# Spreading the steps of a Sinkhorn iteration among matrix products of a fused attention, MLP and expert kernel

## The chip, the cores and the metric

The kernel runs on one core of a Trainium2 chip. The metric is the device time of one execution in microseconds (us); the kernel before was run three times for it. A profiled execution of the same program gives the trace that is read below. The engines are TensorE (PE for its matmuls, PEld for its weight loads), VectorE (DVE), ScalarE (ACT), GpSimd (POOL) and SyncE (SP), which issues the DMA transfers of this kernel.

## The reference

Three stages follow each other: attention with pooled keys and values, an MLP with ELU, and a mixture of eight experts whose gates are balanced by eight rounds of a Sinkhorn iteration.

```python
def _moe2_ref(x, w_gate, w1, w2):          # x: 2304 x 512, w1: 8 x 512 x 1024
    logits = x @ w_gate
    logits = logits - logits.max()
    P = np.exp(logits)
    for _ in range(8):
        P /= P.sum(1, keepdims=True) + 1e-09
        P /= P.sum(0, keepdims=True) + 1e-09
        P *= N / E
    out = np.zeros((N, D), dtype=np.float32)
    for e in range(E):
        h = np.maximum(x @ w1[e], 0.0)
        ye = h @ w2[e]
        out += P[:, e:e + 1] * ye
    return out
```

The gates `P` are used only in the last line, when an expert's output is added up. The product `x @ w1[e]` does not need them.

## The kernel before

The attention and the MLP run in one loop over `items`, 80 of them: five groups `g` of hidden chunks, five token tiles `t` (four of 512 tokens, one of 256), and the chunks of a group. Each item has the first MLP product (`layer1`, L527, tile `p_<item>`), its ELU (L539, L540 on ACT, L547 on DVE), a split into a high and a low part `h` (L548 on ACT, L549 on DVE), and, two items later, the second product (`layer2`, L560, tiles `p_<item>_<j>`). In the last group (g is 4, items 60 to 79) the outputs of a token tile are complete after its four items; `finish2` adds them into `x2a[t]` (L582 on DVE).

From there on work of a second kind exists, kept as a queue of Python generators named `side`. Each `yield` is a place where the queue can be left and entered again. `advance(n)` takes n steps from the front of the queue. For every token tile the queue gets `gate_tile(t)`, which computes the gate logits by matmuls of 8 columns (L442, tile `pg`), and some `halve(t, u)`, which split the tile into the high and low operands `xs` of the next stage (L628 on ACT, L629 on DVE, with differences at L639 to L648). After the last tile it gets `sinkhorn()`.

`sinkhorn()` takes the maximum of all logits (L459 on DVE, a transpose `pmx` at L462, `pmb` at L468 on PE), then the exponential (L471 on ACT), and then eight rounds. A round is a chain on DVE that normalises the rows (L476 to L479), one matmul with a matrix of ones that forms the column sums and gives them to all partitions (`pcs`, L483 on PE), and a chain on DVE that normalises the columns (L486 to L493). Each part needs the one before it.

The next stage, the first pass over the experts, forms `x @ w1[e]` by a scheme of seven products for four blocks. Its unit of work is a `Unit(i, u)`: weight pair i of 32 and token block u of 3. The products run in the order 1, 6, 3 of the unit before, 2, 7, 5, 4, six matmuls each (L713; banks `pa`, `pb`, `pc`, `pd`); product 7 adds to the bank `pb` after product 6 has been read from it (`read`, L732 on DVE), product 2 to `pa` after ACT has read product 1 (L729). Four units of pairs 0 and 1 come first, on token blocks 0 and 1, then pairs 0 and 1 on block 2, then pair 2 on the blocks 0, 1, 2, and so on. After each product the loop calls `advance(2)`. `need(u)` takes steps until the operands of block u exist. After the fifth unit (n is 4) the loop empties the queue:

```python
        if n == 2 * NUNIT - 2:
            advance(10**6)
            load_pair(2)
            load_pair(3)
```

The weights of a pair are loaded by SP (tile `rw`), combined on POOL (L683 to L686), and split into `w` by ACT (L690) and POOL (L691). All large tiles share 24 slots, so a load waits until another tile is given up.

The second pass multiplies by `w2` (L794) and applies the gates; it starts late in the run, and first reads the gates at 1286.8 us of the trace.

The code is written down in the order of these calls; a scheduler then orders each engine's instructions by that order and by what it takes to be ready. Afterwards each engine works through its list in order.

Of the kernel before, what the change touches and what calls it, by code (L numbers as in the profile page):

```python
# [17 lines left out]
def tile_attention_mlp_moe(  # L18
# [34 lines left out]
    E, _, F = w1.shape  # L53
# [14 lines left out]
    G0 = len(SPLIT)  # L68
# [5 lines left out]
    NUNIT = NT // 2 // UW  # L74
# [25 lines left out]
    def bank(name):  # L100
        return psum.tile([P, 512], F32, tag="ps", name=name)
# [326 lines left out]
    def advance_attention(upto):  # L428
        while tick[0] <= min(upto, max(ticks)):
            for step, u in ticks.get(tick[0], []):  # L430
                step(u)
            tick[0] += 1


    def gate_tile(t):
# [17 lines left out]
        )  # L453
        yield

    def sinkhorn():
        NS = NT // P
        mx = cpool.tile([P, 1], F32, name="gmx")
        nc.vector.reduce_max(mx, logits, axis=AX.XY)  # L459
        yield  # L460
        ps = bank("pmx")
        nc.tensor.transpose(ps[0:1, 0:P], mx, ident)  # L462
        m1 = cpool.tile([1, 1], F32, name="gm1")
        nc.vector.tensor_reduce(m1, ps[0:1, 0:P], axis=AX.X, op=ALU.max, negate=True)
        yield
        yield
        ps = bank("pmb")
        nc.tensor.matmul(ps[:, 0:1], ones[0:1, :], m1, start=True, stop=True)  # L468
        nm = cpool.tile([P, 1], F32, name="gnm")
        nc.vector.tensor_copy(nm, ps[:, 0:1])  # L470
        nc.scalar.activation(gates, logits, AF.Exp, bias=nm)  # L471
        rs = cpool.tile([P, NS, 1], F32, name="grs")
        cs = cpool.tile([P, 1, E], F32, name="gcs")
        yield
        for it in range(8):
            nc.vector.reduce_sum(rs, gates, axis=AX.X)  # L476
            nc.vector.tensor_scalar_add(rs, rs, 1e-9)  # L477
            nc.vector.reciprocal(rs, rs)
            nc.vector.tensor_mul(gates, gates, rs.to_broadcast([P, NS, E]))  # L479
            yield  # L480
            yield
            ps = bank(f"pcs{it}")
            nc.tensor.matmul(  # L483
                ps[:, 0 : NS * E], ones, gates.rearrange("p s e -> p (s e)"), start=True, stop=True
            )
            nc.vector.reduce_sum(  # L486
                cs.rearrange("p o e -> p (o e)").unsqueeze(2),
                ps[:, 0 : NS * E].rearrange("p (s e) -> p e s", e=E),
                axis=AX.X,
            )  # L490
            nc.vector.tensor_scalar_add(cs, cs, 1e-9)
            nc.vector.reciprocal(cs, cs)
            nc.vector.scalar_tensor_tensor(  # L493
                gates,
                gates,
                float(NT) / E,
                cs.to_broadcast([P, NS, E]),
                op0=ALU.mult,
                op1=ALU.mult,
            )  # L500
            yield
# [4 lines left out]
    def advance(n=1):  # L506
        for _ in range(n):
            while side:
                try:
                    next(side[0])  # L510
                    break
                except StopIteration:
                    side.pop(0)
# [60 lines left out]
    def finish2(g, t, ps):  # L574
        n = WIDTH[t]
        if g == 0:
            x2a[t] = slot([P, NC, n], F32, f"x2a{t}")
            for j in range(NC):
                nc.scalar.copy(x2a[t][:, j, :], ps[j][:, 0:n])
        else:  # L580
            for j in range(NC):
                nc.vector.tensor_add(x2a[t][:, j, :], ps[j][:, 0:n], x2a[t][:, j, :])  # L582
        if g == G0 - 1:
            del xh[t], xl[t]
            side.append(gate_tile(t))
            side.extend(halve(t, u) for u in AFTER[t])
            if t == NTILE - 1:
                side.append(sinkhorn())
# [7 lines left out]
    CUTS = {}  # L596
# [8 lines left out]
    made = set()  # L605
# [64 lines left out]
    def load_pair(i):  # L670
        e, f = pairs[i]
        raw1[i] = slot([P, 8, 2, P], F32, f"rw{i}")
        for place, hh, kh in ((A11, 0, 0), (A12, 0, 1), (A21, 1, 0), (A22, 1, 1)):
            o = (hh * NPAIR + f) * P
            nc.sync.dma_start(
                raw1[i][:, place],
                w1[e][kh * 2 * P : (kh + 1) * 2 * P, o : o + P].rearrange("(c p) f -> p c f", p=P),
            )

    def split_pair(i):  # L680
        raw = raw1.pop(i)
        g = nc.gpsimd
        g.tensor_add(raw[:, S1], raw[:, A21], raw[:, A22])  # L683
        g.tensor_sub(raw[:, S2], raw[:, S1], raw[:, A11])
        g.tensor_sub(raw[:, S3], raw[:, A11], raw[:, A21])  # L685
        g.tensor_sub(raw[:, S4], raw[:, A12], raw[:, S2])  # L686
        w1s[i] = [slot([P, 7, 2, P], F32R, f"w1{l}_{i}") for l in range(2)]
        for js in (slice(0, 3), slice(3, 5), slice(5, 7)):
            rs = slice(js.start + 1, js.stop + 1)
            nc.scalar.copy(w1s[i][0][:, js], raw[:, rs])  # L690
            g.tensor_sub(w1s[i][1][:, js], raw[:, rs], f32(w1s[i][0][:, js]))  # L691
# [61 lines left out]
    def load_w2(e, q):  # L753

        raw2[e, q] = slot([P, 2, 2, DM], F32, f"rv{e}_{q}")
        rows = w2[e].rearrange("(h f p) d -> f p h d", h=2, p=P)
        for i in range(2):
            nc.sync.dma_start(raw2[e, q][:, i], rows[2 * q + i])
# [81 lines left out]
    def pause(i, left):  # L840


        g, t, f = items[min(i, len(items) - 1)]
        rate = 0.0
        if g == 0:
            for u in range(t + 1, NTILE):
                runs = ((u - t) * SIZE[0] - f - 1) * 4 + left
                rate = max(rate, (ready[u] - tick[0] + 1) / max(runs, 1))
        credit[0] += rate
        n = int(credit[0])  # L850
        credit[0] -= n
        if n:
            advance_attention(tick[0] + n - 1)
        else:
            advance()

    def drive(gen, i, left):
        while True:
            try:
                next(gen)  # L860
            except StopIteration:
                return
            pause(i, left)
# [38 lines left out]
    for i in range(len(items) + LAG):  # L902
        if i < len(items):
            g, t, f = items[i]
            if g == 0:
                advance_attention(ready[t])
            if t == 0:
                finish_chunks(FIRST[g] + f)
            if (g, t, f) == (G0 - 1, NTILE - 1, 0):
                load_pair(0)  # L910
            drive(layer1(i), i, 3)
            pause(i, 2)
        if i >= LAG:
            drive(layer2(i - LAG), i, 1)
            pause(i, 0)
            finish1(i)
            g, t, f = items[i - LAG]
            if t == NTILE - 1:
                done.add(FIRST[g] + f)
            if i > 3:  # L920
                step_chunks()
        else:
            finish1(i)
        if i == len(items) - 2:
            split_pair(0)
            load_pair(1)


    def need(u):
        while not all(k in made for k in CUTS if k[1] == u):  # L930
            advance()
# [5 lines left out]
    for n, (i, u) in enumerate(order1):  # L937
        need(u)
        unit = Unit(i, u)
        for m in (1, 6, None, 2, 7, 5, 4):  # L940
            if m is not None:
                unit.product(m)
                unit.read(m)
            elif last is not None:
                last.product(3)
                last.read(3)
                if last.u == NUNIT - 1:
                    del w1s[last.i]
            advance(2)
        last = unit  # L950
        if n == 2 * NUNIT - 2:
            advance(10**6)
            load_pair(2)
            load_pair(3)
        if n >= 2 * NUNIT - 1 and u == NUNIT - 1 and i + 1 < len(pairs):
            split_pair(i + 1)
            if i + 3 < len(pairs):
                load_pair(i + 3)
        if (i, u) == (len(pairs) - 1, 0):
            load_w2(0, 0)  # L960
# [73 lines left out]
```

## Time and profile before

| | |
|---|---|
| three runs | 2053.34, 2054.75, 2055.7 us; median 2054.75 us |
| profiled execution | 2061.65 us, of which the span from first to last instruction is 2059.9 us |
| PE busy | 1996.6 us, 97% of the span |
| DVE, ACT, POOL busy | 49%, 33%, 20% |
| mean granted TensorE clock | 0.984 of full speed |
| place of the gates' iteration | 555.6 us (maximum of the logits) to 607.1 us (last column step) |

The times of a stage are read from the start of the span. Busy shares are averages over stages with different limits, so a stage has to be looked at by itself.

### The profile page before, as it was taken

The numbers are of one execution on the slowest core, as the hardware profiler recorded it, in microseconds if no ns is written. First come the engines' busy times: TensorE is split into PE (matmuls) and PEld (weight loads), VectorE is DVE, ScalarE is ACT, GpSimd is POOL, SyncE is SP. The second block draws the span as 40 slices with busy tenths as digits, with TensorE's granted clock in tenths as the row PEclk, the third lists the DMA queues.
The fourth block names the chain that finished last, engine by engine and source line by source line (L and its number), as shares of the span: only waits on it lengthen the run. The fifth ranks groups of instructions, "written<-read, shape, count | busy, mean of one in ns | idle before, by whom it ended". The sixth has DMA issues, their size and how long they took to land.

```text
span 2059.9 us, 27328 instructions
## 1 busy us (share of the span) xinstructions
PE 1996.6 (97%) x10139; PEld 1769.9 (86%) x10139; DVE 1008.5 (49%) x1877; ACT 671.9 (33%) x1361; POOL 408.2 (20%) x443
## 2 busy tenths in 40 slices
PE   4899999999969999999999999999999999999999
PEld 3578888888959999999999999888888888888887
DVE  7978878436653333333333334334434443434443
ACT  4665445335312222121122123442323232323221
POOL 5810000002023333333333231210202020202000
PEclk9899999999969999999999999999999999999999
DMA  8321111000123334334334338332424233342311
GB/s 207 98 95 62 62 41 42 0 21 1 50 69 131 137 131 136 134 129 138 130 126 144 130 134 294 144 133 92 141 99 150 92 133 109 117 146 95 123 43 50
DMA packets 138198, 222.00 MB, mean 108 GB/s; under 512 B 14417, under 2 KB 108625, under 8 KB 138065
## 3 DMA queue, kind: packets, MB, share of 16 engines
q1 hardware_dynamic: 138064, 220.26, 31.6%
q8 instruction: 79, 1.29, 0.3%
q14 instruction: 55, 0.44, 0.1%
HBM read 140.00 MB, written 80.22 MB: 107 GB/s over the span
## 4 chain that ended last, share of the span: by engine, by line
PE 71%; DVE 1%; POOL 0%; issue 0%; ACT 0%; DMA 0%; ACTq 0%
PE po L794 38%; PE pb L713 9%; PE pa L713 9%; PE pc L713 9%; PE pd L713 5%; PE pcs L483 0%; POOL w L691 0%; DVE gates L479 0%; DVE grs L477 0%; DVE c L743 0%; DVE acc L821 0%; ACT w L690 0%; DVE gates L493 0%; DVE grs L476 0%; DMA hid<-c 0%
## 5 line engine op out<-in xcount | busy, mean ns | idle before, releaser
L794 PE MATMUL po<-w,g 128*128 128x512 f32 x3456 | 783.9, 389 | 0.4 <-DVE g L780 0.4
L794 PEld LDWEIGHTS po<-w,g 128*128 128x128 f32 x3456 | 648.8, 188 | 135.2 <-DVE g L780 0.9
L780 DVE SCALAR_TENSOR_TENSOR g<-hl,g 128x384 fp32r<-128x384 f32 x384 | 232.6, 607 | 446.8 <-PE po L794 414.1
L779 ACT ACTIVATE g<-hl 128x384 fp32r<-128x384 f32 x384 | 201.8, 526 | 521.4 <-PE po L794 518.0
L713 PE MATMUL pb<-xs,w 128*128 128x384 f32 x1152 | 234.9, 338 | 1.8 <-ACT xs L628 1.8
L713 PE MATMUL pc<-xs,w 128*128 128x384 f32 x1152 | 233.7, 337 | 1.1 <-DVE c L743 1.1
L713 PE MATMUL pa<-xs,w 128*128 128x384 f32 x1152 | 234.3, 338 | 0.2 <-ACT m L729 0.2
L560 PE MATMUL p<-h,w 128*128 128x512 f32 (+1 forms) x960 | 213.8, 370 | 0.0
L691 POOL TENSOR_TENSOR w<-rw,w 128x512 fp32r<-128x512 f32 (+1 forms) x96 | 139.0, 1475 | 375.6 <-ACT w L690 334.6
L713 PEld LDWEIGHTS pb<-xs,w 128*128 128x128 f32 x1152 | 205.7, 191 | 2.2 <-ACT xs L628 2.2
L713 PEld LDWEIGHTS pc<-xs,w 128*128 128x128 f32 x1152 | 204.5, 190 | 1.9 <-DVE c L743 1.9
L713 PEld LDWEIGHTS pa<-xs,w 128*128 128x128 f32 x1152 | 205.3, 190 | 0.5 <-ACT m L729 0.5
L766 POOL TENSOR_TENSOR w<-rv,w 128x512 fp32r<-128x512 f32 x64 | 92.9, 1479 | 555.8 <-ACT w L765 533.3
L560 PEld LDWEIGHTS p<-h,w 128*128 128x128 f32 x960 | 167.1, 189 | 29.7 <-issue 0.5
L527 PE MATMUL p<-xh,w 128*128 128x512 f32 x512 | 172.9, 396 | 0.1
L729 ACT COPY m<-pa 128x384 f32<-128x384 f32 x96 | 46.2, 482 | 333.6 <-PE pa L713 314.1
L743 DVE TENSOR_TENSOR c<-pc,u 128x384 f32<-128x384 f32 x192 | 107.0, 557 | 84.4 <-PE pc L713 84.4
L732 DVE TENSOR_TENSOR u<-pb,m 128x384 f32<-128x384 f32 x96 | 53.5, 557 | 153.3 <-PE pb L713 144.2
L739 DVE TENSOR_TENSOR u<-pb,m 128x384 f32<-128x384 f32 x96 | 53.5, 558 | 141.0 <-PE pb L713 141.0
L685 POOL TENSOR_TENSOR rw<-rw 128x256 f32<-128x256 f32 x32 | 23.7, 740 | 486.2 <-DMA rw<-in_moe_w_dram 424.3
L713 PE MATMUL pd<-xs,w 128*128 128x384 f32 x576 | 116.2, 336 | 0.0
L527 PEld LDWEIGHTS p<-xh,w 128*128 128x128 f32 x512 | 97.1, 190 | 19.9 <-ACT w L142 0.3
(119 smaller groups left out, 1720.1 us busy)
## 6 DMA issues: line engine op xcount, KB each, us to landing
hid<-c SPq DMA_DIRECT2D x384, 192.0 KB
hl<-hid SPq DMA_DIRECT2D x96, 768.0 KB
rw<-in_moe_w_dram SPq DMA_DIRECT2D x128, 128.0 KB
rv<-in_moe_w_dram SPq DMA_DIRECT2D x32, 512.0 KB
raw<-in_moe_w_in_dram SPq DMA_DIRECT2D x16, 512.0 KB
raw<-in_moe_w_out_dram SPq DMA_DIRECT2D x16, 512.0 KB
k<-in_k_dram SPq DMA_DIRECT2D x16, 288.0 KB
v<-in_v_dram SPq DMA_DIRECT2D x16, 288.0 KB
```

Of the source, the lines that this page charges most:

```text
L527: nc.tensor.matmul(ps[:, 0:n], wc[:, 0, a, c * P : (c + 1) * P], b[:, c, :], start=c == 0 and m == 0, stop=c == NC - 1 and m == 2,)
L560: nc.tensor.matmul(ps[j][:, 0 : WIDTH[t]], wc[:, 1, a, j * P : (j + 1) * P], h[b], start=f == 0 and m == 0, stop=f == SIZE[g] - 1 and m == 2,)
L691: g.tensor_sub(w1s[i][1][:, js], raw[:, rs], f32(w1s[i][0][:, js]))
L713: nc.tensor.matmul(self.bank[b], a[:, c, :], x, start=first and c == 0 and n == 0, stop=c == 1 and n == 2, skip_group_check=not first,)
L729: nc.scalar.copy(self.m1, p["a"])
L732: nc.vector.tensor_add(self.u2, p["b"], self.m1)
L739: nc.vector.tensor_add(self.u3, p["b"], self.m1)
L743: nc.vector.tensor_add(v, p[PRODUCTS[m][2]], getattr(self, with_))
L766: nc.gpsimd.tensor_sub(lo, src, f32(hi))
L779: nc.scalar.activation(hi, v, AF.Relu)
L780: nc.vector.scalar_tensor_tensor(lo, v, 0.0, f32(hi), op0=ALU.max, op1=ALU.subtract)
L794: nc.tensor.matmul(outs[k][s], h[a][:, s * P : (s + 1) * P], w2s[e, f][:, hh, b, :], start=first and n == 0, stop=last and n == 2,)
```

## The change

Three places change. Inside `sinkhorn()` the steps are set further apart by a generator `lull()` of six yields: after the maximum, before the second part of it, and in each round between the row part and the column sums. In the last group of the MLP the loop takes two steps of the queue at a time where it took one. In the first pass two steps are taken after a product only while operands are missing, and one afterwards; the call that emptied the queue after the fifth unit becomes `need(NUNIT - 1)`, which only asks for the operands of the last token block. The line numbers of the kernel shift by 2 to 4.

```diff
+    def lull():
+        for _ in range(6):
+            yield
+
     def sinkhorn():
         NS = NT // P
         mx = cpool.tile([P, 1], F32, name="gmx")
         nc.vector.reduce_max(mx, logits, axis=AX.XY)
-        yield
+        yield from lull()
         ps = bank("pmx")
         nc.tensor.transpose(ps[0:1, 0:P], mx, ident)
         m1 = cpool.tile([1, 1], F32, name="gm1")
         nc.vector.tensor_reduce(m1, ps[0:1, 0:P], axis=AX.X, op=ALU.max, negate=True)
-        yield
-        yield
+        yield from lull()
...
             nc.vector.tensor_mul(gates, gates, rs.to_broadcast([P, NS, E]))
-            yield
-            yield
+            yield from lull()
             ps = bank(f"pcs{it}")
...
         if n:
             advance_attention(tick[0] + n - 1)
         else:
-            advance()
+            advance(2 if g == G0 - 1 else 1)
...
-            advance(2)
+            advance(2 if len(made) < len(CUTS) else 1)
         last = unit
         if n == 2 * NUNIT - 2:
-            advance(10**6)
+            need(NUNIT - 1)
             load_pair(2)
             load_pair(3)
```

On PE, at the end of the fifth unit, the list of before has the last product `pd` of that unit and then five column sums in a row, with nothing between them.

```order
L483 MATMUL pcs_5298<-gates,ones 128x144
L713 MATMUL pd_2_5304<-xs_4_5059,w_0_4684 128x384
L713 MATMUL pd_2_5304<-xs_5_5060,w_0_4684 128x384
L713 MATMUL pd_2_5304<-xs_4_5059,w_0_4685 128x384
L713 MATMUL pd_2_5304<-xs_5_5060,w_0_4684 128x384 x2
L713 MATMUL pd_2_5304<-xs_5_5060,w_0_4685 128x384
L483 MATMUL pcs_5318<-gates,ones 128x144
L483 MATMUL pcs_5328<-gates,ones 128x144
L483 MATMUL pcs_5338<-gates,ones 128x144
L483 MATMUL pcs_5348<-gates,ones 128x144
L483 MATMUL pcs_5358<-gates,ones 128x144
L713 MATMUL pa_2_5375<-xs_0_5055,w_1_4785 128x384 x2
```

In the changed kernel the same unit ends with `pd`, and one column sum stands after the next unit's product 1 (`pa`) and ahead of its product 6 (`pb`).

```order
L715 MATMUL pd_2_5278<-xs_4_4902,w_0_4771 128x384
L715 MATMUL pd_2_5278<-xs_5_4903,w_0_4770 128x384 x2
L715 MATMUL pd_2_5278<-xs_5_4903,w_0_4771 128x384
L715 MATMUL pa_2_5299<-xs_0_4898,w_1_4861 128x384 x2
L715 MATMUL pa_2_5299<-xs_0_4898,w_1_4862 128x384
L715 MATMUL pa_2_5299<-xs_0_4898,w_1_4861 128x384 x2
L715 MATMUL pa_2_5299<-xs_0_4898,w_1_4862 128x384
L485 MATMUL pcs_5308<-gates,ones 128x144
L715 MATMUL pb_2_5314<-xs_3_4901,w_1_4861 128x384 x2
L715 MATMUL pb_2_5314<-xs_3_4901,w_1_4862 128x384
```

The other seven column sums follow at the same place of the next seven units, seven products apart.

On PE in the last group of the MLP, the gate matmuls of a token tile stood in pieces of four (one 128-token block), each between six matmuls of an MLP product:

```order
L442 MATMUL pg_4127<-wg,x2a_1238 128x8 x4
L527 MATMUL p_67_4135<-xh_635,w_3409 128x512
L527 MATMUL p_67_4135<-xl_636,w_3409 128x512
L527 MATMUL p_67_4135<-xh_635,w_3409 128x512 x2
L527 MATMUL p_67_4135<-xl_636,w_3409 128x512
L527 MATMUL p_67_4135<-xh_635,w_3409 128x512
L442 MATMUL pg_4127<-wg,x2a_1238 128x8 x4
```

Now they stand in two pieces of eight. That holds for the tiles 0, 1 and 2; for tile 3, whose gates stood in two pieces of eight inside the first pass, the pieces are now of four, eight and four, among the products of the MLP's last item.

```order
L442 MATMUL pg_4111<-wg,x2a_1238 128x8 x8
L562 MATMUL p_64_0_4120<-h_64_4036,w_3060 128x512
L562 MATMUL p_64_0_4120<-h_64_4037,w_3060 128x512
L562 MATMUL p_64_0_4120<-h_64_4036,w_3060 128x512
L562 MATMUL p_64_1_4121<-h_64_4036,w_3060 128x512
L562 MATMUL p_64_1_4121<-h_64_4037,w_3060 128x512
L562 MATMUL p_64_1_4121<-h_64_4036,w_3060 128x512
L442 MATMUL pg_4111<-wg,x2a_1238 128x8 x8
```

On ACT the splits of the first two weight pairs (`w_0`, `w_1`) stood among the items 71 to 73. In the changed kernel they stand among the items 76 and 77, close to the end of the MLP, and the split of pair 1 is ahead of item 77's high part `h_77`.

```order
L692 CAST w_0_4770<-rw_4600 128x768
L550 CAST h_76_4624<-m_4626 128x256
L692 CAST w_0_4770<-rw_4600 128x512 x2
L541 ACTIVATE m_4677<-p_77_4658 128x256
L542 ACTIVATE m_4677<-m_4677 128x256
L630 CAST xs_4_4541<-t_2_1_4682 128x256 x2
L692 CAST w_1_4861<-rw_4778 128x768
L692 CAST w_1_4861<-rw_4778 128x512
L630 CAST xs_2_4539<-x2a_1706 128x256 x2
L692 CAST w_1_4861<-rw_4778 128x512
L630 CAST xs_3_4540<-t_2_1_4709 128x256 x2
L550 CAST h_77_4675<-m_4677 128x256
```

What moved with it is the operands' work (`xs`): the steps of tile 2 for the second token block stand here now, where they stood inside the first pass before.

## Rows read from the trace of the kernel before

**Rows 1.** The page: PE's line, and its clock in 40 slices (tenths).

```profile
PE 1996.6 (97%) x10139; PEld 1769.9 (86%) x10139; DVE 1008.5 (49%) x1877; ACT 671.9 (33%) x1361; POOL 408.2 (20%) x443
PEclk9899999999969999999999999999999999999999
```

**Rows 2.** Windows: length, busy PE, PEld, DVE, ACT, POOL; clock, DMA share, GB/s.

```profile
444.00:528.00 84.00, 84.00 (x465) 73.17 (x464) 48.93 (x97) 39.31 (x93) 12.35 (x10) 1.00 0.02 7
...
527.95:611.01 83.06, 62.56 (x297) 59.10 (x297) 54.10 (x155) 19.89 (x61) 13.00 (x15) 0.75 0.19 65
545.00:553.00 8.00, 8.00 (x35) 8.00 (x35) 2.12 (x7) 0.95 (x3) 0.00 (x0) 0.57 0.15 54
565.00:570.00 5.00, 2.76 (x13) 1.84 (x11) 5.00 (x17) 2.57 (x10) 0.00 (x0) 0.94 0.47 148
588.00:610.00 22.00, 8.17 (x24) 6.87 (x25) 13.17 (x40) 0.98 (x2) 6.75 (x7) 0.54 0.11 34
611.00:1000.00 389.00, 389.00 (x2247) 389.00 (x2246) 148.92 (x267) 83.32 (x161) 129.94 (x125) 1.00 0.39 133
```

**Rows 3.** Windows of L713, L442, L483 alone: PE, PEld, clock, DMA.

```profile
527.95:611.01 83.06, 52.82 (x228) 48.72 (x229) 0.75 0.19 65
...
527.95:611.01 83.06, 6.12 (x48) 6.51 (x48) 0.75 0.19 65
...
527.95:611.01 83.06, 5.92 (x16) 4.11 (x16) 0.75 0.19 65
```

**Rows 4.** The waits of PE between 500 and 640: total, times, longest.

```profile
PE pcs L483 <- DVE gates L479: 17.6, 6, 4.0
```

**Rows 5.** Timeline of column sums and one round: start, length, instruction, [idle before].

```profile
579.19 0.51 PE L483 MATMUL pcs<-gates,ones 128*128 128x144 f32 x2 [2.56 <-DVE gates L479]
...
600.64 0.30 DVE L476 TENSOR_REDUCE grs<-gates 128x18 f32<-128x144 f32 x1
...
601.85 0.85 PE L483 MATMUL pcs<-gates,ones 128*128 128x144 f32 x2 [2.38 <-DVE gates L479]
602.73 0.31 DVE L486 TENSOR_REDUCE gcs<-pcs 128x8 f32<-128x144 f32 x1 [0.94 <-PE pcs L483]
...
603.52 0.31 DVE L493 SCALAR_TENSOR_TENSOR gates<-gates,gcs 128x144 f32<-128x144 f32 x1
```

**Rows 6.** Timeline of the steady first pass: product 6, its read, product 7.

```profile
833.58 1.20 PE L713 MATMUL pb<-xs,w 128*128 128x384 f32 x6
...
834.87 0.56 DVE L732 TENSOR_TENSOR u<-pb,m 128x384 f32<-128x384 f32 x1 [1.58 <-PE pb L713]
...
836.70 1.20 PE L713 MATMUL pb<-xs,w 128*128 128x384 f32 x6
```

**Rows 7.** Timeline of PE at the gate matmuls of tile 3.

```profile
541.53 1.85 PE L442 MATMUL pg<-wg,x2a 128*128 128x8 f32 x16
...
543.24 1.29 PE L713 MATMUL pa<-xs,w 128*128 128x384 f32 x6
...
544.36 2.37 PE L442 MATMUL pg<-wg,x2a 128*128 128x8 f32 x16
```

**Rows 8.** Timeline of the MLP's end: tile 3's addition, last products, last low part.

```profile
513.97 0.69 DVE L582 TENSOR_TENSOR x2a<-p,x2a 128x512 f32<-128x512 f32 x1 [1.41 <-PE p L560]
...
523.68 4.48 PE L560 MATMUL p<-h,w 128*128 128x256 f32 x36
...
525.64 0.43 DVE L549 TENSOR_TENSOR h<-m,h 128x256 fp32r<-128x256 f32 x1 [0.47 <-ACT h L548]
```

**Rows 9.** Timeline of a round's row part beside the weight split on POOL.

```profile
587.54 4.32 POOL L691 TENSOR_TENSOR w<-rw,w 128x768 fp32r<-128x768 f32 x3 [10.20 <-ACT w L690]
587.61 1.77 DVE L477 TENSOR_SCALAR grs<-grs 128x18 f32<-128x18 f32 x1
...
589.71 1.02 DVE L479 TENSOR_TENSOR gates<-gates,grs 128x144 f32<-128x144 f32 x1
```

**Rows 10.** Timeline of POOL: its wait for the load of a weight pair.

```profile
595.27 0.72 POOL L685 TENSOR_TENSOR rw<-rw 128x256 f32<-128x256 f32 x1 [3.41 <-DMA rw<-in_moe_w_dram]
```

## Prediction, made before the changed kernel ran

> **What bounds the kernel now.** I read the page first. PE is busy for 97% of the span, and the clock's slices are at 9 (90% or more of full speed) but for one 8 at the start and one 6 in the middle [rows 1]. So PE sets the time, and a change pays only where PE idles or is slow. The windows then show the place: from 444 to 528 us PE is busy all the time at clock 1.00, from 611 to 1000 again, and in the 83.06 us between 527.95 and 611.01 it is busy for 62.56 at a mean clock of 0.75 [rows 2]. The waits of PE name the cause: six times a column sum waited for a row chain on DVE, 17.6 us together [rows 4]. A round shows why: the row chain starts at 600.64, the column sum at 601.85, the column chain runs from 602.73 to 603.83, and then the next row chain begins; PE has nothing else in its list meanwhile [rows 5]. From 588 to 610 PE was busy for 8.17 of 22 us, at clock 0.54, close to the lower level of 1.2 GHz [rows 2].
>
> **What the stretch would cost without waits.** Between 527.95 and 611.01 PE ran 228 matmuls of products (38 products of six), 48 matmul instructions for gates and 16 for column sums [rows 3]. In the steady pass 2247 product matmuls take 389.00 us, 0.1731 us each or 1.04 per product [rows 2]: 228 x 0.1731 = 39.5 us. Sixteen gate instructions take 1.85 us at full clock, 0.116 each [rows 7]: 48 x 0.116 = 5.6. A column sum is a pair of instructions; the trace has pairs of 0.51 and 0.85 us, the second at low clock [rows 5]: 8 x 0.51 = 4.1. No row has one inside a dense run at full clock; half of 0.51 is my lower end (2.0 for eight), 0.85 the upper (6.8). I take 0.51, the row with the higher clock. The two small matmuls for the maximum I put at 0.9 together, three instructions at some 0.3. Sum: 50.1 us. Of the 83.06 us 33.0 are lost to waits and low clock, with bounds of 30.3 and 35.1.
>
> **What the change gives back.** In the new list one column sum comes per unit, and six products stand between a row chain and the column sum that needs it. The row chain takes 1.2 us [rows 5]; the six products, 6.2 us, hide it. The column sum itself stays on PE and is in the 50.1. The column chain (1.1 us) starts when the sum is done and ends about when product 6, 1.04 us long, ends, so it hardly delays that product's read; the row chain comes behind that read. In the steady pass the read of product 6 ends at 835.43 and product 7 starts at 836.70, so DVE has 1.27 us to spare there [rows 6]. Reads that come later in a unit may slip by 1.2 us and catch up: DVE is busy for 148.92 of 389 us in the steady pass [rows 2], 2.8 of 7.3 us a unit, and a round adds 2.3. The gates are first used in the second pass, 680 us after the iteration's end, so their lateness (some 50 us) costs nothing. The burst of operand work ahead of the fifth unit also ends: from 565 to 570 us PE was busy for 2.76 of 5 us while DVE was busy all the time [rows 2]; in the new list this work is done two units earlier. All of this is in the 33.0 us.
>
> **What it adds.** Three costs, none of them shown as such.
>
> First, the gate matmuls in larger pieces. After 16 gate instructions, one product, and 16 gate instructions [rows 7] the granted clock fell: 0.57 over 545 to 553 us [rows 2], which is some 6.9 us at 1.2 GHz, half of it lost, 3.4 us. That loss is in the 33.0, and it can come back: the tiles 0, 1 and 2 now have this pattern with a half MLP product between the pieces, and tile 3 has pieces of 8, 16 and 8 instructions with six 256-column matmuls between. In pieces of eight, as they stood for the tiles 0 to 2, the clock stayed at 1.00 [rows 2]. Bounds: no fall, and four falls of 3.4, 13.6 us. Tile 3 is nearest to the row; I take one fall, 3.4.
>
> Second, the end of the MLP. The queue runs twice as fast there, so DVE and ACT get more work between 444 and 528. They were busy for 48.93 and 39.31 of 84 us [rows 2]; what moves in from the first pass is some 13 us on DVE. On average there is room. At the end it is tight: in before there were 12.1 us from tile 3's addition at 513.97 to the last low part at 526.07 [rows 8], and PE needed that part for the last 12 of the 36 instructions that start at 523.68. The splits of the first weight pairs now queue there on ACT as well, ahead of `h_77`. In return the list puts more than one product of the first unit ahead of the last MLP products. Between nothing and 6 us; I take 1.
>
> Third, DVE in the first two units, where a tile's remaining operand work (near 13 us) meets the reads of products, and the meetings with POOL. Beside a weight split on POOL one DVE instruction took 1.77 us and one 1.02 [rows 9], in a chain that takes 1.2 us as a whole elsewhere [rows 5]. POOL is busy for 129.94 of 389 us in the steady pass [rows 2], so about three of eight rounds meet it; a column chain longer by 2.3 us would hold back product 7 by 2.3 - 1.27, some 1 us. Between nothing and 4 us; I take 1. The Trainium skill, SBUF — State Buffer, section "Who interferes with whom", says that some VectorE instructions and GpSimd exclude each other for a whole instruction. Its rule speaks against the change, since the rounds now run beside POOL's steady work; the trace agrees, with the 1.77 us. If every one of a round's DVE instructions were held for one POOL instruction, the term would go to its upper end of 4 us and the sum would be 24.6 in place of 27.6.
>
> **Sum.** 33.0 - 3.4 - 1 - 1 = 27.6 us gained. The profiled execution took 2061.65 us (span 2059.9 and 1.75 around it), so 2034.0 for it; it stands 6.9 us above the median, 2054.75, which I take as the spread of executions. From the median: 2054.75 - 27.6 = 2027.2 us.
>
> **The rivals.** *More falls of the clock:* at all four gate tiles. For it: the pieces are as large as those of [rows 7]; against it: between them stand longer runs than in that row for three tiles. 10.2 us more: 2037.4.
>
> *A new wait at the end of the MLP:* pair 1's load can start only when tile 1's `x2a` is given up, POOL waited 3.41 us for such a load [rows 10], and its split takes 4.32 us [rows 9]; ACT would hold `h_77` behind it, and PE would wait. Against it: the load is freed near item 76, several us before. With a fall of the clock after the wait 3.4 + 3.4, less the 1 counted: 2033.
>
> *The rounds stall PE all the same, and the kernel is slower:* if each column sum waits for its chain, the clock falls again each time, as at 588 to 610 [rows 2], and now 56 products stand between the first sum and the last. At 1.2 GHz each costs 1.04 us more, 58 us against the gain of 27.6: 2085. It decides from some 27 products at low clock. Against it: the chain would have to grow from 1.2 us past the 6.2 of its cover, and even beside POOL it took 3.5. The Trainium skill, TensorE: Matmul & The Clock Gate, section "A second HAM failure mode: psum-queue depth-cycling", tells of short idle times between groups of matmuls that send the clock back and forth; by it the waits here need not be long. In this trace the falls in the rounds came with waits of 2.4 us and more.
>
> *The change doesn't spread the steps:* the list shows single column sums, so only if PE's time is lost elsewhere to the same amount: 2054.
>
> **Chances.** The forecast 0.80, with a range of its own of 2020 to 2033; more falls 0.07; the wait at the end of the MLP 0.06; slower 0.04; no change 0.03. A measurement of this kernel tells 0.2% (4 us) from no change. Faster 0.93, same 0.03, slower 0.04. The range: 35.1 us with no new cost gives 2019.7; 30.3 less 13.6 gives 2038. So 2020 to 2038, which leaves out the last two cases and the tails.
>
> **What would show it.** Right: PE busy near 100% from 528 on, the wait of column sums for L479 (now L482) gone, eight single column sums about 7.8 us apart, the mean clock over 0.99, the last product of the first pass some 28 us earlier, nothing different in the second pass. The first cost shows as a clock of 0.5 for some 7 us behind a gate piece between 450 and 530; the second as PE idle for L560 or for `w` near 525; the third as PE idle for the read at L732 (now L734). The forecast is wrong if column sums still wait, if the clock is under 1 over several units after 560, or if the first unit starts more than 6 us later than the moved gate matmuls of tile 3 (3.7 us) explain.

## The result, and the profile after

The changed kernel takes 2030.12 us (median of 4 runs, 2028.16 to 2033.97), beside 2054.05 for the kernel before on the same chip (2051.88 to 2055.7): a ratio of 0.9886, 95% interval 0.9868 to 0.9904. 2027.2 had been predicted. The profiled execution took 2029.24 us, with a span of 2027.5.

The page, PE's line and its clock in 40 slices:

```profile
PE 1987.7 (98%) x10139; PEld 1763.3 (87%) x10139; DVE 1003.7 (50%) x1877; ACT 670.5 (33%) x1361; POOL 411.0 (20%) x443
...
PEclk9899999999899999999999999999999999999999
```

In [rows 1] the twelfth of the slices was a 6. Now there is an 8, one slice earlier: the place of the loss has moved. The windows, with the columns of [rows 2], show both places:

```profile
444.00:515.10 71.10, 71.10 (x376) 61.05 (x374) 41.34 (x89) 32.95 (x84) 10.11 (x10) 1.00 0.05 16
515.00:520.00 5.00, 2.28 (x14) 1.84 (x13) 4.62 (x7) 1.75 (x4) 4.90 (x5) 0.85 0.00 0
518.00:532.00 14.00, 12.68 (x56) 12.69 (x57) 9.60 (x20) 5.47 (x18) 3.21 (x3) 0.52 0.00 1
535.00:611.00 76.00, 75.74 (x446) 74.83 (x446) 50.80 (x130) 21.20 (x52) 24.54 (x25) 1.00 0.37 124
611.00:1000.00 389.00, 389.00 (x2248) 389.00 (x2247) 152.78 (x286) 81.68 (x159) 127.15 (x124) 1.00 0.39 133
```

From 535 on PE is busy for 75.74 of 76 us at clock 1.00, where it had been 62.56 of 83.06 at 0.75. The steady pass is as it was. But at the end of the MLP, where PE had been busy all the time [rows 2], it now idles for 2.7 of the 5 us from 515 to 520, and then runs for some 13 us at 0.5, the lower level of 1.2 GHz.

All waits of PE from 440 to 640 (total, times, longest), and below them the column sum at 580.55 with the products around it:

```profile
PE pg L442 <- DVE x2a L584: 2.1, 1, 2.1
PE p L562 <- DVE x2a L584: 0.6, 1, 0.6
PE pb L715 <- DVE u L734: 0.3, 1, 0.3
```

```profile
579.68 1.03 PE L715 MATMUL pa<-xs,w 128*128 128x384 f32 x5
580.55 0.41 PE L485 MATMUL pcs<-gates,ones 128*128 128x144 f32 x2
580.70 1.30 PE L715 MATMUL pb<-xs,w 128*128 128x384 f32 x6
581.83 1.20 PE L715 MATMUL pc<-xs,w 128*128 128x384 f32 x6
582.87 1.20 PE L715 MATMUL pa<-xs,w 128*128 128x384 f32 x6
```

The 17.6 us of [rows 4] are gone, and no column sum waits. Eight of them stand 7.5 to 8.1 us apart from 573.02 to 626.24. A pair lasts 0.41 us in the trace, but costs PE less, because it overlaps its neighbours: the product behind it starts 0.15 us after it, and the next product 1.13 us after that one, where 1.04 is usual. So a sum in a dense run costs 0.15 + 0.09 = 0.24 us.

**A measure without the attention.** The first stage differs from one execution to the next: tile 0's first addition in the last group of the MLP (L584, L582 before) starts at 443.89 in the profile of before and at 437.03 here. The very first addition of the MLP, at 187.3 and 180.4, is as far apart already, and two profiles of the changed kernel itself differ by 4.1 us there (441.16 in e9, below). The comparisons below therefore also use the *tail*, from that start to the end of the span: 2059.9 - 443.89 = 1616.0 before, 2027.5 - 437.03 = 1590.5 after. The change gives back 25.5 us there.

| kernel | first addition | span | tail | median time |
|---|---|---|---|---|
| before | 443.89 | 2059.9 | 1616.0 | 2054.05 |
| after | 437.03 | 2027.5 | 1590.5 | 2030.12 |
| after, again (e9) | 441.16 | 2031.9 | 1590.7 | 2031.83 |
| gates later (e1) | 440.06 | 2031.6 | 1591.5 | 2033.62 |
| slow last tile (e2) | 441.62 | 2031.1 | 1589.5 | 2032.11 |
| before, no rounds (e3) | 441.23 | 2025.6 | 1584.4 | 2026.87 |
| after, no rounds (e4) | 437.23 | 2025.5 | 1588.3 | 2028.47 |
| weights early (e5) | 442.27 | 2023.5 | 1581.2 | 2024.35 |
| weights early, again (e10) | 436.31 | 2020.7 | 1584.4 | 2022.65 |
| one weight late (e11) | 442.34 | 2023.8 | 1581.5 | 2024.06 |
| spread alone (e6) | 436.73 | 2021.8 | 1585.1 | 2023.99 |
| drain kept (e7) | 438.01 | 2053.4 | 1615.4 | 2053.45 |
| lull of two (e12) | 436.55 | 2033.6 | 1597.1 | 2036.21 |
| lull of one (e8) | 439.74 | 2039.5 | 1599.8 | 2041.36 |

The two profiles of the changed kernel start the tail 4.1 us apart, and their tails agree within 0.3 us. Each tail comes from one profile, though, and that of before is from an execution (2061.65 us) longer than any of its timed runs. Measured against before, the gains by the tails are 0.2 to 5.3 us larger than by the medians, so the tails are best compared among the changed versions. The median of e7 is over ten runs, one of which took 2234.23 us at a mean granted clock of 0.843, a slower state of the chip.

**The end of the MLP.** PE, DVE and POOL in the timeline of the changed kernel:

```profile
515.80 0.62 PE L562 MATMUL p<-h,w 128*128 128x256 f32 x3 [0.65 <-DVE x2a L584]
516.40 0.83 PE L442 MATMUL pg<-wg,x2a 128*128 128x8 f32 x6
519.32 0.60 PE L442 MATMUL pg<-wg,x2a 128*128 128x8 f32 x2 [2.08 <-DVE x2a L584]
519.76 1.63 PE L529 MATMUL p<-x,w 128*128 128x256 f32 x6
521.19 3.42 PE L442 MATMUL pg<-wg,x2a 128*128 128x8 f32 x16
```

```profile
509.90 1.78 DVE L641 TENSOR_TENSOR t<-x2a 128x512 f32<-128x512 f32 x1
511.61 0.68 DVE L584 TENSOR_TENSOR x2a<-p,x2a 128x512 f32<-128x512 f32 x1
...
516.73 1.93 DVE L631 TENSOR_TENSOR xs<-x2a,xs 128x256 fp32r<-128x256 f32 x1 [0.38 <-ACT xs L630]
518.58 0.68 DVE L584 TENSOR_TENSOR x2a<-p,x2a 128x512 f32<-128x512 f32 x1
...
528.15 0.42 DVE L631 TENSOR_TENSOR xs<-x2a,xs 128x256 fp32r<-128x256 f32 x1 [3.89 <-ACT xs L630]
```

```profile
507.84 5.00 POOL L693 TENSOR_TENSOR w<-rw,w 128x768 fp32r<-128x768 f32 x3 [43.74 <-ACT w L692]
...
516.57 4.63 POOL L693 TENSOR_TENSOR w<-rw,w 128x768 fp32r<-128x768 f32 x3
```

The last of these splits in the kernel before:

```profile
504.81 4.45 POOL L691 TENSOR_TENSOR w<-rw,w 128x768 fp32r<-128x768 f32 x3 [13.79 <-issue]
```

PE's gates need tile 3's four additions (L584). In DVE's list operand work of tile 2 stands between them, and the last of it, at 516.73, took 1.93 us; without POOL beside it, at 528.15, the same step takes 0.42. POOL worked there from 507.84 to 521.20 with only the weights of the pairs 0 and 1, the splits of both and, between them, the combining of pair 1. It had done them by 509.3 in the kernel before; counted from tile 0's first addition that is 65.4 us, against 84.2 here. The steps of DVE that were stretched here take both inputs from SBUF (L631, L641); the additions, with one input from a PSUM bank, took 0.68 as elsewhere. The Trainium skill, SBUF — State Buffer, section "Who interferes with whom", makes this distinction: a DVE instruction with two inputs in SBUF contends with a GpSimd instruction that reads SBUF, one with at most one such input does not, outside some modes. This trace agrees, with 1.93 against 0.68.

### The profile page after: what moved, and what is told of

Same layout as the page of the kernel before. It is cut to its first block, busy times and chain, and to the rows that moved or that the text cites. A ratio compares the mean times of both kernels' runs of the same rounds, so it can differ in the third digit from the quotient of the medians.

```text
span 2027.5 us, 27333 instructions
## 1 busy us (share of the span) xinstructions
PE 1987.7 (98%) x10139; PEld 1763.3 (87%) x10139; DVE 1003.7 (50%) x1877; ACT 670.5 (33%) x1361; POOL 411.0 (20%) x443
## 4 chain that ended last, share of the span: by engine, by line
PE 93%; DVE 4%; DMA 1%; ACT 1%; POOL 1%; issue 0%; SPq 0%; DVEq 0%; ACTq 0%; POOLq 0%
PE po L796 39%; PE pa L715 10%; PE pb L715 10%; PE pc L715 10%; PE p L562 9%; PE p L529 9%; PE pd L715 5%; PE pg L442 1%; DVE k L290 1%; DMA raw<-in_moe_w_out_dram 0%; DVE sm L288 0%; POOL w L693 0%; PE px L322 0%; DMA v<-in_v_dram 0%; PE pt L295 0%
```

## The experiments

**Gates later (e1).** Is it the wait that brings the clock down, or the gate matmuls?

```diff
     def gate_tile(t):
-        for _ in range(4):
+        for _ in range(8 if t == 3 else 4):
             yield
```

> The changed kernel, with tile 3's gate matmuls four queue steps later; DVE's list stays nearly as it is. In the changed kernel PE waited 0.65 and 2.08 us for tile 3's addition (L584) and then ran at half clock from 518.3 to 532, some 6.8 us lost. Theory 'wait': the clock fell because of the waits; without the 2.08 it stays at 1.00, and the run gives 2030.1 - 2.1 - 6.8 = 2021. Theory 'pieces': the 8-column matmuls themselves bring the clock down, wherever they stand; the wait goes, a stretch at 0.5 of 10 us or more stays behind the pieces, and the run gives 2028.

2033.62 us (2031.18 to 2033.85), ratio 0.9895 (0.9878 to 0.9911); tail 1591.5. Neither theory held. The wait did not go, it was shared out and grew, from 2.7 to 4.4 us. PE from 440 to 700:

```profile
PE p L562 <- ACT h L550: 2.5, 1, 2.5
PE pg L442 <- DVE x2a L584: 1.3, 1, 1.3
PE p L562 <- DVE x2a L584: 0.6, 1, 0.6
```

From 524 to 538 the mean clock was 0.52. So moving the instruction that waits does not help, where what it waits for is late.

**Slow last tile (e2).**

```diff
-            advance(2 if g == G0 - 1 else 1)
+            advance(2 if g == G0 - 1 and t < NTILE - 1 else 1)
```

> The changed kernel, with two queue steps a pause only while the tiles 0 to 3 are in work; during the last tile's items one step, as before the change. On DVE the four additions of tile 3 then stand ahead of tile 2's operand work, and its gate matmuls move into the first unit of the first pass, in pieces of 12 and 4. Theory 'wait': no wait of over 0.5 us at the end of the MLP, clock at 1.00, 2030.1 - 2.7 - 6.8 = 2020.6. Theory 'pieces': the waits go, but the clock falls behind the piece of 12, at some 530, for 7 us or more: 2024 to 2027.

2032.11 us (2028.98 to 2034.8), ratio 0.989 (0.9875 to 0.9905); tail 1589.5. The waits did not go, against both theories: tile 3's addition was in time, and PE waited for the two parts of h instead:

```profile
PE p L562 <- DVE h L551: 2.0, 1, 2.0
PE p L562 <- ACT h L550: 1.3, 1, 1.3
```

The clock was at 0.57 from 526 to 530, behind these waits, at 1.00 from 530 to 536, and at 0.57 again from 536 to 544, although PE was busy throughout from 530 on. This second fall stands behind 24 gate instructions in one piece. They are the 12 matmuls of the expectation: the trace has two instructions for each gate matmul of the list (32 for the 16 of tile 3), and so the pieces of 4, 8 and 4 are 8, 16 and 8 in the trace. The fall that "pieces" expected came, but its time did not. e1 and e2 have one thing in common with the changed kernel: the weight splits stay at the end of the MLP, on POOL and ACT.

**The rounds left out, before (e3) and after (e4).** In both `for it in range(8)` becomes `for it in range(0)`.

> The kernel before, with the eight rounds left out (the gates are then the bare exponentials). It measures the drain by itself. Theory of the prediction: of the 33.0 us lost between 528 and 611, 3.4 belong to the gates' fall of the clock and 2.2 to the operands' burst at 565 to 570, so the rounds' waits and low clock are 27.4, and the column sums themselves 4.1: 2054.1 - 31.5 = 2022.6. Rival: the waits only move (operand work and slots are late as well), and no more than 20 us go: 2034 or above.

> The changed kernel, with the eight rounds left out (the gates are then the bare exponentials). It measures what the spread rounds still cost. Theory 'nearly free': eight column sums of 0.15 to 0.28 us in PE's list and one wait of 0.26: 1.5 to 2.5 us, 2027.6 to 2028.6, and so slower than the kernel before without its rounds by the 6 us or so that are lost at the end of the MLP. Rival, the prediction's own prices: 4.1 for the column sums and 1 for meetings with POOL, 2025.

e3: 2026.87 us (2025.93 to 2031.99), tail 1584.4, which is 31.6 us below before; 31.5 were expected. By the medians it is 27.6 (2054.5 - 2026.87), so the time of 2022.6 was missed by 4.3, and the rival's 2034 by more. e4: 2028.47 us (2027.3 to 2030.45), tail 1588.3, 2.2 us below after, within the 1.5 to 2.5 of "nearly free"; eight sums at 0.24 us and the one wait of 0.26 make the same 2.2. So by the tails the eight rounds cost 31.6 us in one go and 2.2 us spread. Without rounds the changed kernel's tail is 3.9 us longer than that of the kernel before, from the end of the MLP; their medians, 1.6 us apart, do not tell them apart.

**Weights early (e5, and again e10).** The loads and splits of the pairs 0 and 1 are called earlier; nothing else.

```diff
-            if (g, t, f) == (G0 - 1, NTILE - 1, 0):
+            if (g, t, f) == (G0 - 1, 2, 0):
                 load_pair(0)
+            if (g, t, f) == (G0 - 1, 2, 3):
+                split_pair(0)
+                load_pair(1)
+            if (g, t, f) == (G0 - 1, 3, 2):
+                split_pair(1)
...
-        if i == len(items) - 2:
-            split_pair(0)
-            load_pair(1)
...
-    split_pair(1)
     last = None
```

> The changed kernel, with the loads and splits of the first two weight pairs written earlier, so that they stand among the items 67 and 68 of ACT's list, and nothing of them among the last items; PE's list keeps tile 3's gate matmuls in pieces of 4, 8 and 4. In the two runs before, the wait at the end of the MLP did not go, it moved from tile 3's addition to the low and high part of h, and the clock fell with it. Theory 'weights': the weight splits on POOL and ACT are what holds DVE and ACT there; without them PE waits less than 0.5 us, the clock stays at 1.00, and from tile 0's first addition to the end it takes 1590.5 - 2.7 - 6.8 = 1581 us, a time of some 2021. Theory 'pieces': the waits go, but the clock still falls behind the gate pieces: 1587.8, a time of 2027.

> The kernel with both weight pairs' loads and splits written earlier, again, beside the changed kernel. Theory: no wait of PE over 0.5 us between 440 and 700, clock 1.00 at the gate pieces of 8, 16 and 8, 1581 us from tile 0's first addition to the end, 5 to 8 us less than the changed kernel: 2023 to 2025. Rival: the clock stayed up by chance in the first profile, and falls here behind the gate pieces although PE doesn't wait: 1585 to 1588.

e5: 2024.35 us (2023.01 to 2025.27), ratio 0.9857 (0.9837 to 0.9878), tail 1581.2, as "weights" expected, though the time is 3 us above its 2021. e10: 2022.65 us (2022.24 to 2025.05), ratio 0.9848 (0.9831 to 0.9865), tail 1584.4; the changed kernel beside it (e9) took 2031.83. PE of e5 at the same gate matmuls, and the window around them:

```profile
520.60 0.96 PE L442 MATMUL pg<-wg,x2a 128*128 128x8 f32 x8
521.41 0.96 PE L529 MATMUL p<-x,w 128*128 128x256 f32 x6
522.21 1.85 PE L442 MATMUL pg<-wg,x2a 128*128 128x8 f32 x16
```

```profile
505.00:535.00 30.00, 30.00 (x208) 28.17 (x207) 19.65 (x52) 14.55 (x45) 0.00 (x0) 1.00 0.01 1
```

PE waits nowhere there, the clock is at 1.00, and POOL is idle. The weights are the cause of the waits. But in e10, the same program, the clock did fall, although PE was busy throughout:

```profile
516.25 2.11 PE L442 MATMUL pg<-wg,x2a 128*128 128x8 f32 x16
518.21 1.63 PE L529 MATMUL p<-x,w 128*128 128x256 f32 x6
```

```profile
517.00:518.00 1.00, 1.00 (x9) 1.00 (x10) 0.65 (x2) 0.00 (x0) 0.00 (x0) 0.85 0.00 0
518.00:522.00 4.00, 4.00 (x20) 4.00 (x21) 0.52 (x2) 0.61 (x3) 0.00 (x0) 0.50 0.00 0
522.00:524.00 2.00, 2.00 (x11) 2.00 (x11) 1.24 (x4) 1.79 (x7) 0.00 (x0) 0.50 0.00 0
524.00:525.00 1.00, 1.00 (x6) 1.00 (x6) 1.00 (x4) 0.97 (x3) 0.00 (x0) 0.74 0.00 0
```

Six us at 0.50 and the parts of the two at 0.85 and 0.74 make some 6.8 us at the lower level; the tail is 3.2 us longer than that of e5, about half of that time. So the rival of e10's expectation was right as well: the gate pieces alone bring the clock down in some executions, at 3.2 us, and not in others (e5 and e10 ran on two different chips).

**One weight late (e11).** The edit of e5, with `split_pair(0)` and `load_pair(1)` at (G0 - 1, 3, 0), and `split_pair(1)` where it was.

> Half the suspected cause: pair 0's load and splits written earlier, pair 1's still among the items 76 and 77. Theory 'POOL beside DVE': what holds DVE is the length of POOL's bursts; with one split (4.6 us) instead of two the waits fall below 1 us, the clock stays, 1581 to 1584 us from tile 0's first addition to the end: 2025. Theory 'ACT': pair 1's splits on ACT stand ahead of h_77 and are enough; a wait of 1.5 us or more stays and the clock falls behind it: 1588 to 1591, 2030.

2024.06 us (2022.54 to 2025.58), ratio 0.9852 (0.9835 to 0.987), tail 1581.5: no wait over 0.2 us, clock 1.00 over 505 to 535. The theory "ACT" fails. DVE and POOL there:

```profile
519.36 0.68 DVE L584 TENSOR_TENSOR x2a<-p,x2a 128x512 f32<-128x512 f32 x1
...
520.97 4.65 POOL L693 TENSOR_TENSOR w<-rw,w 128x768 fp32r<-128x768 f32 x3 [48.52 <-issue]
...
521.44 3.05 DVE L631 TENSOR_TENSOR xs<-t,xs 128x256 fp32r<-128x256 f32 x2
524.41 1.49 DVE L551 TENSOR_TENSOR h<-m,h 128x256 fp32r<-128x256 f32 x1
```

POOL still holds DVE: three steps take 4.5 us that take some 1.2 without it. But tile 3's last additions are done before the burst starts. So it was not the size of the burst that mattered here, but what stood behind it in DVE's list.

**Spread alone (e6).** `advance(2 if g == G0 - 1 else 1)` becomes `advance()` again; the rest of the change stays.

> The change without its faster queue in the last group of the MLP: one step a pause there, as before. Theory: the whole gain is the spread of the rounds; the end of the MLP is then as in the kernel before, with the fall of the clock at tile 3's gates and the 1.8 us for operands, and from tile 0's first addition to the end it takes 1584.4 (the kernel before without rounds) + 2 = 1586.5 us, 4 less than the changed kernel. Rival: the operands of the last block come late without the faster queue, PE waits for them: 1595 or more.

2023.99 us (2023.57 to 2025.78), ratio 0.9859 (0.9834 to 0.9884); tail 1585.1, 5.4 us less than the changed kernel. The size is that of the theory, its makeup is not. The windows of e6 at tile 3's gates, in pieces of 16, and at the operands' burst:

```profile
534.00:545.00 11.00, 11.00 (x83) 11.00 (x82) 5.61 (x17) 1.76 (x5) 0.00 (x0) 1.00 0.20 72
555.00:560.00 5.00, 2.72 (x14) 2.08 (x14) 4.96 (x16) 2.90 (x11) 0.00 (x0) 1.00 0.52 165
560.00:564.00 4.00, 4.00 (x16) 4.00 (x15) 1.39 (x4) 0.52 (x2) 2.81 (x4) 0.57 0.67 203
```

The gates' fall of the clock, expected from [rows 7], did not come in this execution; the burst's wait of 2.3 us did, as in [rows 2], with a short fall behind it. The faster queue removes this wait, and buys a larger one: without it POOL is done with the weights of the pairs 0 and 1 at 502.1, 65.4 us behind tile 0's first addition, as in the kernel before. So the faster queue is what moved them, and as the change has it, it costs more than it brings: e6 is 5.4 us shorter than the changed kernel by the tails, and all its runs are below all of the changed kernel's. A fall at the gates, had it come, would have taken some 3 us of that (an estimate, from the 3.2 us of e10).

**Drain kept (e7).** `need(NUNIT - 1)` becomes `advance(10**6)` again.

> The changed kernel, with the call that empties the queue after the fifth unit put back. Theory: the drain is the cause of the loss; nearly all eight rounds still stand one behind the other there, the waits of the column sums are 15 us or more again, and the gain goes: 2052 to 2058. Rival: the longer gaps between the steps and the faster queue help by themselves, so that half of the gain or more stays: 2042 or less.

2053.45 us (median), ratio 0.9996 (0.9983 to 1.0008); tail 1615.4. The whole gain goes:

```profile
PE pcs L485 <- DVE gates L482: 19.1, 7, 3.3
```

**Shorter lulls (e8 one step, e12 two).** `for _ in range(6)` in `lull()` becomes `range(1)` and `range(2)`.

> The changed kernel, with a lull of one step instead of six: one product (1.04 us) between a row chain and its column sum, a round every two products. Theory 'cover': the row chain takes 1.2 us and DVE has reads to do as well, so each column sum waits 0.3 to 1.5 us, 2 to 12 us in all, and the clock stays near 1.00: 2032 to 2042. Rival 'clock': short waits at every second product bring the clock down over some 17 products, 17 us more: 2050 or above. Third: the queue in front of PE hides it, no wait, 2030.

> The changed kernel, with a lull of two steps: two products, 2.1 us, between a row chain of 1.2 us and its column sum, a round every three products. With one step the run lost 9.3 us from tile 0's first addition to the end. Theory 'cover': two products are enough, no wait of a column sum over 0.5 us, 1590 to 1593: 2030 to 2033. Rival: it is DVE's total work (reads, operands of the last block and rounds at once) that is late, and waits of 1 us and more stay at several sums: 1595 or more, 2035 or above.

e8: 2041.36 us (2039.46 to 2046.59), ratio 0.9945 (0.9925 to 0.9965), tail 1599.8, 9.3 more than after. That is the time that "cover" gave, but not each sum waited: three of eight did, 0.87, 1.38 and 2.47 us. Ahead of the longest wait no product stands between two sums at all, and it alone was followed by a fall of the clock, to 0.72 on average from 582 to 588:

```profile
578.99 0.51 PE L485 MATMUL pcs<-gates,ones 128*128 128x144 f32 x2
581.97 0.48 PE L485 MATMUL pcs<-gates,ones 128*128 128x144 f32 x2 [2.47 <-DVE gates L482]
```

e12: 2036.21 us (2035.37 to 2038.84), ratio 0.9916 (0.9896 to 0.9936), tail 1597.1, 6.6 more. That is the rival's number, but not its reason: the first five sums did not wait, and the two that did met POOL. The second of them in e12:

```profile
585.93 4.41 POOL L693 TENSOR_TENSOR w<-rw,w 128x768 fp32r<-128x768 f32 x3
...
586.51 1.34 DVE L480 TENSOR_SCALAR grs<-grs 128x18 f32<-128x18 f32 x1
...
588.18 1.02 DVE L482 TENSOR_TENSOR gates<-gates,grs 128x144 f32<-128x144 f32 x1
...
589.26 0.85 PE L485 MATMUL pcs<-gates,ones 128*128 128x144 f32 x2 [2.37 <-DVE gates L482]
```

Two products cover the chain of 1.2 us, but not one that meets a weight split (L480 here has one input only, and was held too). The six of the change cover both: in its own trace a column chain beside POOL took 1.09 and 1.11 us in two of its steps, and product 7 waited 0.26 us.

**After, again (e9).** The changed kernel itself.

> The changed kernel itself, beside the next three runs on one chip. Theory: as before, a wait of 2.1 us for tile 3's addition, some 13 us at half clock behind it, and 1590 us from tile 0's first addition to the end: 2030. Rival: the fall of the clock was chance, and is missing in this profile: 2024.

2031.83 us (2029.97 to 2034.07), tail 1590.7, the same waits of 2.08 and 0.62 us, and 13 us at 0.50 from 524 on. The rival, that the fall was chance, fails.

## Why the prediction was right, and where its sum was off

**What the change gives back:** 33.0 was predicted, with 30.3 and 35.1 as bounds. e5 is the change with nothing lost at the end of the MLP, and its tail is 1616.0 - 1581.2 = 34.8 us shorter than that of before (29.5 by the medians). The row with the column sums was taken too high: in a dense run one costs 0.24 us and not 0.51, eight times 0.27 or 2.2 us less, which turns the 33.0 into 35.2. e7 and e3 show that the drain is the cause, and that the rounds were 31.6 of it by the tails. The mechanism was right.

**First and second cost:** 3.4 for one fall of the clock and 1 for the end of the MLP, 4.4 together. e5 against the changed kernel says 1590.5 - 1581.2 = 9.3 us: 2.7 us of waits, and 12.68 busy us at a mean clock of 0.52, so 12.68 x 0.48 = 6.1 us for the low clock, 8.8 in all. In e10 the first cost stands alone, at 3.2 us, about the 3.4 that had been taken; so it is the second cost, the end of the MLP, that was mis-sized: 1 predicted, some 6 measured. They had been priced as two things and come together here: the wait stands among the gate matmuls, and the clock then stays down for twice as long as behind the pieces alone (13 us against 6.8 in e10). The second cost was rightly placed, and the prediction said of that place that "at the end it is tight". What it missed is that the faster queue also moved the weight splits of both pairs, on POOL, into the same 13 us as tile 2's operand work. The order showed the splits on ACT at the items 76 and 77; POOL's part behind them was priced in the first pass alone.

The rival "a new wait at the end of the MLP", which had 0.06, came true in its place and in its clock fall; the 2030.12 us lie midway between its 2033 and the forecast of 2027.2. Its chain did not come true: PE waited for tile 3's addition on DVE, not for `h_77` behind ACT, and e11, with pair 1's split still ahead of `h_77`, doesn't wait.

**Third cost:** 1 us predicted, 0.3 measured, the one wait of `pb` above. The reserve of [rows 6] and the six products absorb the meetings with POOL; e12 shows that they are real.

**Sum:** 34.8 - 9.3 = 25.5 us by the tails, against 27.6. The medians say 23.9 (2054.05 - 2030.12). That the total is so close is in part luck: the gain was put some 2 us too low, the losses some 4 us too low, and the two errors partly cancel. Of the 6.9 us by which the profiled execution of before stood above its median, a good part lay ahead of tile 0's addition, which came at 443.89; the other profiles, of kernels with the same attention, have it from 436.31 to 442.34, 439.3 on average. Where the rest lay is not shown.

One of the prediction's own signs of being wrong came close. Counted from tile 0's first addition, the first unit starts 9.0 us later than before (530.15 against 528.00 in the traces); the moved gate matmuls explain 3.7 of it, and the remaining 5.3 are just under the limit of 6.

Among the other rivals, "more falls" did not occur at the tiles 0 to 2 (clock 1.00 over 444 to 515.10), and "the rounds stall PE" is what a lull of one or two steps begins to do.

Three versions beat the change as it stands, and the record does not tell them apart: the weights early (2024.35 us, ratio 0.9857, and 2022.65 us, ratio 0.9848), one weight late (2024.06 us, 0.9852) and the spread alone (2023.99 us, 0.9859), where the changed kernel has 0.9886 and 0.9891. The simplest of them leaves the queue as it was.

What stays open: what decides, from one execution to the next, whether the gate pieces alone bring the clock down. That POOL, and not the two splits on ACT together, held DVE is read from the durations (the step at 516.73 took 1.5 us longer than alone, and had waited 0.38 us for ACT) and from e11; a run with POOL's part alone taken away was not made.

## What to carry to other kernels

A serial chain of small steps costs a busy engine next to nothing, if each step is given as much independent work ahead of it as the chain takes *beside the worst neighbour* (here 6.2 us for a chain of 1.2 to 3.5), and it costs its whole length when a queue is emptied in one go. A queue that is run faster moves more than the steps that one looks at: here the loads and splits of weights moved too, so look for where such work lands on every engine, POOL's list included. When a change has several parts, run each alone: here the spread of the rounds brought the whole gain, and the faster queue took some 5 us of it back. Compare two profiles from an event behind any stage that varies by itself; that made differences of 3 us between profiles readable here, in a kernel whose first stage spreads by 7.6.

## What the hardware showed unexpectedly

The clock's fall behind a run of 8-column gate matmuls is not settled by the program alone. In e5 and e10, two profiles of one program with pieces of 8, 16 and 8 instructions, the clock stayed at 1.00 in the first and fell in the second; in e11, with the same pieces, it stayed. With 16 of them, six product matmuls and 16 more, it fell in two executions ([rows 2] for before, and e3, where it was 0.57 from 542 to 550), and stayed at 1.00 in the third (e6, above). In all six profiles with a wait of 2.07 or 2.08 us between such matmuls (after, e4, e7, e8, e9, e12) it fell. What the wait adds to the pieces behind it is not separated by these runs.
